# Slot 2 of a mixture-of-experts kernel: rows turned earlier, its lists split, and the last write of an item moved past a branch

## The chip, the cores and the metric

The kernel runs on 1 core of one Trainium2 chip, as one launch. The metric is the device time in microseconds; lower is better. PE is TensorE, DVE is VectorE, ACT is ScalarE, POOL is GpSimd, SP is SyncE, which here only issues DMAs.

## What is computed

Two stages in float32. First a sparse attention over q, k, v of shape (4 batches, 8 heads, 768 tokens, 64): each token sees the keys closer than 16 positions, and one summary (maximum of keys, mean of values) for every block of 32 tokens.

```
k_sum, v_sum = block max of k, block mean of v          # 24 blocks of 32
scores = [q k^T / 8 where |i-j| < 16, q k_sum^T / 8 + log 32]
x = softmax(scores) @ [v; v_sum]                        # (3072 tokens, 512)
```

Then a routed expert layer over the 3072 tokens of x: every token goes to the one expert of 8 with the largest gate logit.

```
e = argmax(x @ w_gate);  gate = softmax(x @ w_gate)[e]
out = gate * sigmoid(x @ w_output_gate)[e] * (relu(x @ w1[e]) @ w2[e])    # w1: 512x1024, w2: 1024x512
```

Which tokens belong to which expert is known only while the kernel runs.

## The kernel before

**Attention.** 24 tiles of 128 tokens (4 batches of 6). Each goes through scores on PE, mask and row minimum on DVE, subtraction on POOL, exponential on ACT, turning and weighting on PE, normalisation on DVE; the result is stored to DRAM (x_dr) and its gate logits are formed. The order of all these steps, on all engines at once, is written out by hand in the string ORDER: `sc.3:P` is the scores of tile 3 in the PSUM bank pair P, `rk.4.v` reorders a loaded block of k on DVE (`.a` ACT, `.p` POOL), `pu`, `kg` move block means, `lv` loads values, `r` is a step of routing, `sp` splits one weight tile, `ef`, `er`, `e2` are slot 0's two matrix products, `fa` builds four of the 24 "places" matrices (one-hot rows), `fr.2` gathers slot 2's rows. Each engine works through its part of the string in order.

**Slots.** Tokens of one expert are packed into slots of 256 rows. Slots 0 to 2 are formed from the first two batches while attention still runs; slots 3 to 7 follow in straight code; after that items of 256 rows (`full`) and of 128 rows (`half`) alternate inside nested run-time branches (`pairs`, `left`, `more`). In this run there are three of each, slots 8 to 13.

**One slot.** Each weight tile (128x512, 256 KB) comes by a DMA of SP into a ring of raw buffers, is rounded on ACT (w1h, w2h; line 1053) and its remainder formed on DVE (w1l, w2l; line 1054). x rows are gathered by an indirect DMA of POOL (`fetch`, line 1015) into xg, turned on PE (line 1066) and rounded likewise by `take_x` (xhl, lines 1068 and 1069). `first_wide` (lines 1100 and 1102) makes eight hidden blocks j in four PSUM banks, each evicted by ACT and DVE; `second` adds eight blocks of three matmuls for two row tiles (lines 1339 to 1341). At j = 4 of `second` the next slot's rows are turned. `write` scales the result into y and POOL scatters it to out by an indirect DMA (line 1370). In `half` y is scaled half on DVE (line 1364) and half on ACT (line 1365).

**Slot 1** (`full_with`) is ordered by hand as well. Between its products DVE does the remaining routing steps (`rest_slots`) and splits the weights of slots 1 and 2. When the table of the later slots is made, it also issues `final_match` (line 1243, on DVE: which token falls into which list, 24 x 40 entries) and POOL's `final_entries` (line 971, five products of up to 1000 elements). At j = 4 of its second product it turns slot 2's rows.

**Lists.** A slot's row numbers and gates are collected on PE: 24 matmuls of places by entries (`final_collect`, line 1264), then unpacked on DVE (lines 977 to 979). Before, one collection at block 4 of slot 2's first product serves all slots from 3 on; slot 3's rows are fetched at block 6. `few_*` treats two small leftover groups of up to 32 tokens in slots 3 to 7.

**Branches.** Every engine loads the counts and takes each branch for itself (line 1479); line 1536 is the end of the program, where all engines meet. From slot 2 on only POOL's order is as written; the other engines' orders are a scheduler's, except in `half`.

Of the kernel before, what the change touches and what calls it, by code (L numbers as in the profile page):

```python
# [11 lines left out]
F32 = mybir.dt.float32  # L12
F32R = mybir.dt.float32r
BF16 = mybir.dt.bfloat16
# [8 lines left out]
P = 128  # L23
# [40 lines left out]
lk.0 rk.0.v lk.2 lk.1 pk.0.0:P rk.1.v rk.2.a pk.0.1 kk.0 lq.0 pk.2.0:S pk.2.1 lk.3 cl.0 pk.1.0:V lq.1 lk.4 rq.0.a  # L64
pk.1.1 mk.2 mk.0 rq.1.p kk.2 rk.3.p pq.0.0:S pq.0.1 pq.1.0:S lk.5 rk.5.p kk.1 mk.1 kq.0 ks.0.v lq.2 pq.1.1 sc.0:P kq.1
rq.2.p lv.2.0.p pk.3.0:S pk.3.1 hm.16:T ma.0 sc.1:V rk.4.v kk.3 lv.0.0.s lv.1.0.s cl.1 mi.0 pk.5.0:P lv.4.0.s mk.3
ma.1 lq.3 lv.3.0.s pk.5.1 pk.4.0:V pk.4.1 sc.2:S me.0.0 lv.5.0.s su.0 lv.0.1.s mk.5 pq.2.0:S pq.2.1 mi.1 sc.3:P kk.4
ma.2 mi.2 lq.4 ex.0 kk.5 tp.0.0:S su.1 kq.2 lk.7 tp.0.1 me.0.1 rq.3.a ex.1 sc.4:V su.2 mk.4 lv.2.1.s lv.1.1.s ma.3
lq.5 kp.0 me.0.2 tp.1.0:P ex.2 mi.3 lv.9.0.s ma.4 tp.2.0:S tp.2.1 tp.1.1 ke.0 lv.3.1.s mg.0:M pq.3.0:P pq.3.1
lv.10.0.s lv.7.0.p su.3 lk.6 lq.6 kg.0.vvvv kp.1 kp.2 ex.3 ks.1.p lv.6.0.p sc.5:V lq.7 mi.4 hm.20:T kq.3 ma.5 pu.2.a  # L70
mi.5 rq.4.p tp.3.0:S pu.0.v tp.3.1 lv.5.1.s sc.6:V va.0.0:P pu.3.a va.0.1 su.4 pu.4.a va.2.0:V ex.4 va.2.1 sc.7:P
tp.4.0:S ma.6 kp.3 lv.8.0.p pq.4.0:V pq.4.1 no.0 tp.4.1 lv.6.1.s no.2 su.5 pu.1.p lk.8 ex.5 me.1.0 mi.6 tp.5.0:V
tp.5.1 ma.7 rk.7.p tx.0:P va.1.0:S va.1.1 kq.4 va.3.0:V mi.7 kp.4 va.3.1 no.1 sc.8:P lv.11.0.p tx.2:S me.1.1 kp.5
rq.5.p kx.0 kx.2 su.6 tx.1:V st.1.s pu.5.v pq.5.0:S pq.5.1 no.3 me.1.2 ex.6 tp.6.0:S kq.5 st.2.s ma.8 tp.6.1 lv.13.0.s
lv.12.0.s sc.9:V kx.1 rk.6.v lv.4.1.p pk.6.0:P st.0.p lk.9 su.7 ke.1 pk.6.1 mi.8 kp.6 tx.3:S ex.7 tp.7.0:V mg.1:M
va.4.0:S su.8 kx.3 kk.6 va.4.1 kg.1.aaaa lg.1:T tp.7.1 sc.10:P ma.9 mi.9 pk.7.0:S rq.6.p pu.6.p lv.7.1.p lv.9.1.p
st.3.s pk.7.1 kp.7 mk.6 ex.8 lv.14.0.s kl.1 va.5.0:V kk.7 va.5.1 pq.6.0:P no.4 hm.6:T pq.6.1 lg.0:T ma.10 tp.8.0:V
tp.8.1 rk.8.p pu.10.a pu.8.v lv.8.1.s su.9 no.5 va.6.0:P va.6.1 tx.4:S mk.7 kq.6 lv.17.0.s lv.15.0.s rq.7.p sc.11:V
tx.5:S kl.0 mi.10 st.5.s su.10 no.6 kp.8 lk.10 pk.8.0:P kx.4 pk.8.1 lt.0:T tx.6:S me.2.0 pq.7.0:V pu.7.p ex.9 ma.11
pq.7.1 mk.8 tp.9.0:S tp.9.1 va.7.0:P va.7.1 rk.9.v pk.9.0:V kx.5 pk.9.1 ks.2.v lv.16.0.s pu.9.v lt.1:T lq.8 kt.0 ex.10  # L80
lv.10.1.s no.7 kx.6 kk.8 tx.7:P kq.7 kt.1 mi.11 kp.9 kk.9 st.6.s sc.12:S ma.12 st.4.p su.11 mk.9 kx.7 va.8.0:P va.8.1
lg.2:T tp.10.0:S no.8 kl.2 tp.10.1 me.2.1 mi.12 va.9.0:V pu.11.v va.9.1 no.9 kp.10 sc.13:P lv.11.1.s ex.11 rk.10.p
sc.14:S ma.13 lk.11 mi.13 tp.11.0:V tp.11.1 kp.11 me.2.2 ma.14 pk.10.0:P pk.10.1 lt.2:M tx.8:S su.13 mi.14 ke.2 lg.3:T
mg.2:M va.10.0:V va.10.1 kt.2 kk.10 rq.8.p tx.9:S kl.3 st.7.s pq.8.0:P pq.8.1 kx.8 mk.10 no.10 ex.13 lt.3:T va.11.0:V
va.11.1 kx.9 kq.8 su.12 kg.2.vvvv tp.13.0:P ex.12 tp.13.1 sc.16:S tx.10:V no.11 kp.13 lg.4:M tx.11:P pu.13.v kx.10
# [814 lines left out]
class Experts:  # L900
# [296 lines left out]
    def full_with(self, s, rest):  # L1197
# [10 lines left out]
        for j in range(NF):  # L1208
            if j == 4:
                self.take_x(2)  # L1210
# [329 lines left out]
```

## Time and profile before

| | |
|---|---|
| time, median of 3 runs | 494.48 us (494.2 to 495.54) |
| profiled execution's own time | 494.04 us |
| its span, first to last instruction | 492.2 us |
| mean granted TensorE clock | 0.956 of full speed |
| busy in the span | PE 454.3 us (92%), DVE 381.2 (77%), ACT 323.6 (66%), POOL 209.4 (43%) |
| DMA | 113.78 MB, 231 GB/s on average |

The span is the profiled execution without what lies around it (1.84 us). Shares are averages over stages of different kind: attention (to 178 us), slots 0 and 1 (to 213.6), slot 2 (to 248.7), straight slots (to 375), branches. So it is read by stage.

### The profile page before, as it was taken

How to read it: one execution, taken by the hardware profiler on the slowest of the kernel's cores; microseconds unless marked ns; L12 is line 12 of the kernel's file. 1: busy time of each engine (PE TensorE's matmuls, PEld its weight loads, DVE VectorE, ACT ScalarE, POOL GpSimd, SP SyncE). 2: the span in 40 equal slices, each digit the busy share in tenths (PEclk: the TensorE clock that was granted, in tenths of full speed). 3: DMA queues.
4: the chain of work that ended last, by engine and by line, in shares of the span. 5: the costliest groups of instructions: out<-in, count | busy, mean ns of one | idle time of the engine just before them, and what ended most of it. 6: DMA issues, size and time to landing. Idle time of an engine off the chain costs nothing.

```text
span 492.2 us, 13115 instructions
## 1 busy us (share of the span) xinstructions
PE 454.3 (92%) x4647; PEld 370.0 (75%) x4647; DVE 381.2 (77%) x760; ACT 323.6 (66%) x605; POOL 209.4 (43%) x224
## 2 busy tenths in 40 slices
PE   6779899998799999949999999999999999999992
PEld 6646677676577789838888887888877888888881
DVE  1675878999886887999878786678747878978884
ACT  2466588587587664624667676667656777877773
POOL 3387955585876079655321212131202313113112
PEclk9686999999899999977999999999999999999997
DMA  9999999697148897157796962999717699598560
GB/s 229 244 202 190 210 248 238 161 222 163 57 155 306 242 381 258 68 162 244 218 355 229 397 228 82 316 390 381 252 56 271 213 307 328 180 313 318 189 218 28
DMA packets 101514, 113.78 MB, mean 231 GB/s; under 512 B 35634, under 2 KB 60388, under 8 KB 101440
## 3 DMA queue, kind: packets, MB, share of 16 engines
q1 hardware_dynamic: 94624, 94.59, 64.4%
q0 software_dynamic: 6816, 18.27, 11.3%
q8 instruction: 38, 0.62, 0.6%
q14 instruction: 36, 0.29, 0.2%
HBM read 102.70 MB, written 12.98 MB: 235 GB/s over the span
## 4 chain that ended last, share of the span: by engine, by line
PE 52%; DVE 1%; issue 1%; ACT 0%; ACTq 0%; DVEq 0%
PE bank L1100 14%; PE bank L1341 8%; PE bank L1339 8%; PE bank L1340 8%; PE bank L1102 7%; PE bank L1066 2%; PE bank L1293 1%; PE bank L1291 1%; PE bank L1292 1%; PE bank L1462 1%; PE bank L1441 1%; DVE w2l L1054 1%; PE bank L1304 1%; PE bank L1264 0%; DVE xhl L1069 0%
## 5 line engine op out<-in xcount | busy, mean ns | idle before, releaser
L1100 PE MATMUL bank<-xhl,w1h 128*128 128x512 f32 x288 | 106.2, 408 | 7.3 <-DVE xhl L1069 6.8
L1015 POOL DMA_INDIRECT xg<-x_dr,ids x32 | 39.1, 1221 | 99.7 <-PE bank L1066 84.1
L1102 PE MATMUL bank<-xhl,w1l 128*128 128x256 f32 x288 | 81.3, 284 | 0.0
L1339 PE MATMUL bank<-w2h,hh 128*128 128x512 f32 x200 | 80.3, 401 | 0.0
L1340 PE MATMUL bank<-w2l,hh 128*128 128x512 f32 x200 | 78.7, 393 | 0.0
L1341 PE MATMUL bank<-w2h,hl 128*128 128x512 f32 x200 | 77.9, 396 | 0.0
L1100 PEld LDWEIGHTS bank<-xhl,w1h 128*128 128x128 f32 x288 | 55.2, 192 | 21.5 <-DVE xhl L1069 7.2
L1054 DVE TENSOR_TENSOR w2l<-wrawb,w2h 128x512 fp32r<-128x512 f32 x77 | 53.1, 706 | 22.2 <-ACT w2h L1053 19.3
L1053 ACT ACTIVATE w2h<-wrawb 128x512 fp32r<-128x512 f32 x77 | 47.1, 627 | 21.7 <-PE bank L1341 16.4
L1102 PEld LDWEIGHTS bank<-xhl,w1l 128*128 128x128 f32 x288 | 55.6, 193 | 1.2
L492 POOL TENSOR_TENSOR pr<-pr,mn 128x960 f32<-128x960 f32 x24 | 43.2, 1805 | 20.4 <-DVE mn L487 12.0
L1370 POOL DMA_INDIRECT out_dram<-y,ids x25 | 27.7, 1109 | 55.6 <-DVE y L1367 17.0
L1053 ACT ACTIVATE w1h<-wrawb 128x512 fp32r<-128x512 f32 x73 | 42.3, 623 | 10.6 <-PE bank L1100 10.5
L1054 DVE TENSOR_TENSOR w1l<-wrawb,w1h 128x512 fp32r<-128x512 f32 x70 | 46.1, 687 | 2.3 <-ACT w1h L1053 1.0
L1054 DVE TENSOR_TENSOR w2l<-wrawa,w2h 128x512 fp32r<-128x512 f32 x43 | 34.3, 815 | 15.0 <-ACT w2h L1053 12.4
L1341 PEld LDWEIGHTS bank<-w2h,hl 128*128 128x128 f32 x200 | 37.5, 188 | 8.9 <-DVE hl L1307 0.9
L1339 PEld LDWEIGHTS bank<-w2h,hh 128*128 128x128 f32 x200 | 37.6, 188 | 7.6
L1340 PEld LDWEIGHTS bank<-w2l,hh 128*128 128x128 f32 x200 | 37.6, 188 | 7.6
L479 DVE TENSOR_TENSOR pr<-sp,c_sb 128x960 f32<-128x960 f32 x24 | 27.7, 1155 | 15.8 <-PE pt L506 8.3
L1106 ACT ACTIVATE hh<-lo 128x256 fp32r<-128x256 f32 x72 | 28.7, 413 | 16.0 <-DVE lo L1105 12.1
L1105 DVE TENSOR_TENSOR lo<-bank,lo 128x256 f32<-128x256 f32 x72 | 28.9, 418 | 10.0 <-ACT lo L1104 8.7
L1107 DVE SCALAR_TENSOR_TENSOR hl<-lo,hh 128x256 fp32r<-128x256 f32 x72 | 29.3, 421 | 8.9 <-ACT hh L1106 6.4
(261 smaller groups left out, 954.2 us busy)
## 6 DMA issues: line engine op xcount, KB each, us to landing
wrawb<-in_moe_w_dram SPq DMA_DIRECT2D x150, 256.0 KB
wrawa<-in_moe_w_dram SPq DMA_DIRECT2D x82, 256.0 KB
raw_k<-in_k_dram SPq DMA_DIRECT2D x12, 512.0 KB
raw_q<-in_q_dram SPq DMA_DIRECT2D x12, 512.0 KB
vw<-in_v_dram SPq DMA_DIRECT2D x33, 128.0 KB
w1few<-in_moe_w_dram SPq DMA_DIRECT2D x16, 256.0 KB
w2few<-in_moe_w_dram SPq DMA_DIRECT2D x16, 256.0 KB
x_dr<-xs SPq DMA_DIRECT2D x14, 256.0 KB
```

The costliest lines, as they stand in the source:

```text
L492: nc.gpsimd.tensor_tensor(pr, pr, mns.pop(i).unsqueeze(2).to_broadcast([P, H, W]), ALU.subtract)
L1015: nc.gpsimd.indirect_dma_start(out=self.xg[t], out_offset=None, in_=self.x_dr[0:rows, :], in_offset=bass.IndirectOffsetOnAxis(ap=self.entr ...
L1053: nc.scalar.activation(hi, raw, AF.Copy)
L1054: (lo_by or nc.vector).tensor_tensor(lo, raw, hi.bitcast(F32), ALU.subtract)
L1100: nc.tensor.matmul(hp.rearrange("p a n -> p (a n)"), lhsT=w_h[:, fs], rhs=self.x[:, c].rearrange("p a n -> p (a n)"), start=c == 0, stop=F ...
L1102: nc.tensor.matmul(hp[:, 1, :], lhsT=w_l[:, fs], rhs=self.xh[:, c, :], start=False, stop=c == NC - 1)
L1105: nc.vector.tensor_tensor(lo, hp[:, 0, :], lo, ALU.add)
L1106: nc.scalar.activation(hh[:, j, :], lo, AF.Relu)
L1107: nc.vector.scalar_tensor_tensor(hl[:, j, :], lo, 0.0, hh[:, j, :].bitcast(F32), ALU.max, ALU.subtract)
L1339: nc.tensor.matmul(y, lhsT=hh[:, j, tk], rhs=w_h, start=j == 0, stop=False)
L1340: nc.tensor.matmul(y, lhsT=hh[:, j, tk], rhs=w_l, start=False, stop=False)
L1341: nc.tensor.matmul(y, lhsT=hl[:, j, tk], rhs=w_h, start=False, stop=j == NF - 1)
```

## The change

1. In `full_with`, `take_x(2)` moves from j = 4 to j = 1 of the second product, and `final_match` and the five `final_entries` are no longer issued there.
2. The lists are split. Slots 3 to 5 get their own (6 columns): match and entries on DVE and the collection in slot 2, the fetch of slot 3 at block 5. The lists of all later slots (34 columns) are made later: the match on POOL as 24 operations in slot 2, the five entries on POOL one at a time in slots 2, 3 and 4, the collection in slot 4, `few_lists` there too.
3. From slot 7 on, the scatter of an item's last row tile (`y_last`, all of it scaled by ACT) is held back and issued by `send_last` inside the next item's branch, or after all branches; so are the gather of the item after next and the last one (after a full item) or three (after a half item) w2 tiles of the next item.
4. ORDER is replaced by another order of the same 792 steps. Counted by engine: copies of k and q on DVE 5 and 5, on ACT 4 and then 8, on POOL 15 and then 11; copies of means (`pu`) on ACT 11 and then 5, POOL 6 and 14, DVE 7 and 5; `kg` of one batch from DVE to ACT. The order now ends with slot 0's write ahead of the places (`fa`).

```diff
 ORDER = """
-lk.0 rk.0.v lk.2 lk.1 pk.0.0:P rk.1.v rk.2.a pk.0.1 kk.0 lq.0 pk.2.0:S pk.2.1 lk.3 cl.0 pk.1.0:V lq.1 lk.4 rq.0.a
...
-fa.0 sp.v xx.0 xx.2 fr.2 e2.4 e2.5 fa.1 fa.2 e2.6 r.3 sp.v sp.v fa.3 r.3 st.21.s fa.4 sp.v sp.v fa.5 e2.7 r.3 r.3 gp.3
-wr
+hm.6:T lk.1 lk.0 rk.0.a lk.2 rk.1.p rk.2.v lq.0 lq.1 lk.3 rk.3.p lk.4 pk.1.0:V pk.0.0:P rq.0.a pk.0.1 pk.2.0:S pk.1.1
+pk.2.1 pq.0.0:V mk.2 lk.5 pq.0.1 lv.4.0.p lv.2.0.p kk.1 kk.0 mk.1 mk.0 ks.0.v cl.1 lq.2 pk.3.0:S kk.2 lv.3.0.s pk.3.1
+rq.1.v rk.5.v pq.1.0:V kq.0 cl.0 kk.3 mk.3 pq.1.1 lv.0.0.p kq.1 rk.4.a lq.3 lv.1.0.s sc.0:P sc.1:V pk.5.0:P ma.0
...
-CF = 2 * (NITEM - 2) + SMALL
+SOON = 3
+CS = 2 * SOON
+CF = 2 * (NITEM - 2 - SOON) + SMALL
...
 (full_with)
-            if j == 4:
+            if j == 1:
                 self.take_x(2)
...
-                    self.final_match()
-                    for x in range(5):
-                        self.final_entries(x)
...
+    def soon_entries(self):
+        b = self.st.tile([P, H, D], F32, name="soon", tag="xs0", bufs=1).rearrange("p h d -> p (h d)").bitcast(BF16)
+        self.soon_b = b[:, 0:NT * NV * CS].rearrange("p (g v c) -> p g v c", v=NV, c=CS)
+        self.entries(self.tc.nc.vector, self.soon_b, self.matched("soon", slice(0, CS)), 0)
+    def soon_lists(self):
+        e = shaped(self.bank(next(self.turn)), [P, NV, CS])
+        for g in range(NT):
+            self.tc.nc.tensor.matmul(e.rearrange("p v c -> p (v c)"), lhsT=self.place_of(g),
+                                     rhs=self.soon_b[:, g].rearrange("p v c -> p (v c)"), start=g == 0, stop=g == NT - 1)
+        self.unpack(1, e)
     def final_match(self):
-        self.tc.nc.vector.tensor_tensor(self.match, self.rt["key"].unsqueeze(2).to_broadcast(sh), ...
+        for g in range(NT):
+            self.tc.nc.gpsimd.tensor_scalar(self.match[:, g, :], start, self.rt["key"][:, g:g + 1], None, ALU.is_equal)
...
+        part = [lambda x=x: self.final_entries(x) for x in range(5)]
+        return {2: {("first", 1): [self.soon_entries], ("first", 4): [self.soon_lists],
+                    ("first", 5): [lambda: self.fetch(EARLY, 2)], ("second", 0): [self.final_match], ("second", 5): [part[0]]},
+                3: {("first", 1): [part[1]], ("first", 5): [part[2]], ("second", 1): [part[3]]},
+                4: {("first", 1): [part[4]], ("first", 4): [self.final_collect, self.final_lists],
+                    ("first", 5): [self.few_lists]}}
+    def late(self, s, n):
+        return () if s < EARLY + STRAIGHT - 1 else range(NF - 1, NF) if n == 2 else range(NF - 3, NF)
...
 (write)
+            held = s >= EARLY + STRAIGHT - 1 and t == len(yp) - 1
+            y = self.y_last if held else self.mp2.tile([P, DM], F32, name="y", bufs=3)
...
+            if not held:
+                self.send(y, at)
+    def next_item(self, s, n, late):
+        if late is not None:
+            self.fetch(s + 1, 2)
+            self.fetch_w(2, s, late)
+            self.send_last()
+        self.tc.nc.gpsimd.tensor_copy(self.at_last, self.entry(s, n - 1)[0])
...
 (rest)
         self.pairs(EARLY + STRAIGHT, 0, *n)
+        self.send_last()
```

`next_item` is called at the head of `full` (from slot 7 on; slot 7 only copies its row numbers) and of `half`. `fetch(nxt2, 2)` in the middle of an item stays only in slots before 7.

## Rows read from the trace of the kernel before

**Rows 1.** Windows: length, busy us (instructions) of PE, PEld, DVE, ACT, POOL; clock; DMA share; GB/s.

```profile
0.00:50.00 50.00, 39.60 (x565) 30.77 (x565) 27.28 (x32) 26.28 (x33) 28.74 (x39) 0.76 1.05 216
...
120.00:132.00 12.00, 8.12 (x178) 5.83 (x174) 11.62 (x36) 6.21 (x8) 7.64 (x11) 0.96 0.13 37
...
190.00:213.60 23.60, 23.60 (x154) 21.27 (x152) 21.11 (x86) 13.61 (x27) 15.36 (x27) 1.00 0.29 95
...
248.70:375.00 126.30, 125.92 (x806) 104.12 (x804) 92.75 (x184) 83.80 (x182) 26.54 (x24) 1.00 0.75 266
375.00:482.60 107.60, 107.50 (x540) 89.17 (x540) 88.65 (x162) 81.30 (x169) 27.76 (x23) 1.00 0.75 255
...
222.00:225.00 3.00, 3.00 (x11) 2.52 (x11) 3.00 (x3) 0.00 (x0) 3.00 (x2) 0.50 0.83 311
```

**Rows 2.** Timeline of PE, slots 1 to 3: start, us, instruction, idle before.

```profile
213.36 0.39 PE L1341 MATMUL bank<-w2h,hl 128*128 128x512 f32 x1
220.52 0.80 PE L1100 MATMUL bank<-xhl,w1h 128*128 128x512 f32 x1 [6.77 <-DVE xhl L1069]
...
226.84 0.40 PE L1100 MATMUL bank<-xhl,w1h 128*128 128x512 f32 x1
...
229.31 1.29 PE L1264 MATMUL bank<-entries,places 128*128 128x200 bf16 x13
...
248.73 0.39 PE L1100 MATMUL bank<-xhl,w1h 128*128 128x512 f32 x1
```

**Rows 3.** Timeline of DVE, slots 1 and 2.

```profile
213.58 1.15 DVE L1243 TENSOR_TENSOR match<-key,startb 128x960 bf16<-128x960 f32 x1
...
219.79 1.27 DVE L1069 TENSOR_TENSOR xhl<-bank,xhl 128x512 fp32r<-128x512 f32 x2
...
226.86 0.74 DVE L1367 TENSOR_SCALAR y<-bank,gates 128x512 f32<-128x512 f32 x1
```

**Rows 4.** Lines of DVE, 214.5 to 226.5: count | busy us, mean ns | idle.

```profile
L1054 DVE TENSOR_TENSOR w2l<-wrawa,w2h 128x512 fp32r<-128x512 f32 x5 | 8.6, 1773 | 0.0
...
L1069 DVE TENSOR_TENSOR xhl<-bank,xhl 128x512 fp32r<-128x512 f32 x2 | 1.3, 674 | 0.0
```

**Rows 5.** Lines of POOL, 189 to 226.

```profile
L965 POOL TENSOR_SCALAR places<-c_sb,rowof 128x128 bf16<-128x128 bf16 x20 | 13.2, 672 | 0.0
L971 POOL TENSOR_TENSOR entries<-match,vals 128x1000 bf16<-128x1000 bf16 x4 | 9.0, 2286 | 8.2 <-DVE match L1243 8.2
```

**Rows 6.** Timeline of PE, from slot 3 to slot 4.

```profile
271.59 0.39 PE L1100 MATMUL bank<-xhl,w1h 128*128 128x512 f32 x1
...
272.53 0.62 PE L1341 MATMUL bank<-w2h,hl 128*128 128x512 f32 x2
```

**Rows 7.** Lines of DVE, 132 to 178: slot 0's list entries.

```profile
L971 DVE TENSOR_TENSOR entries<-match,vals 128x360 bf16<-128x360 bf16 x1 | 1.2, 1180 | 0.0
```

**Rows 8.** Timeline of PE, 140 to 143.5: the collection of the first lists.

```profile
141.16 0.47 PE L1001 MATMUL entries<-entries,places 128*128 128x30 bf16 x12
```

**Rows 9.** Lines of DVE, 189 to 206, while POOL builds places.

```profile
L1054 DVE TENSOR_TENSOR w1l<-wrawb,w1h 128x512 fp32r<-128x512 f32 x4 | 2.9, 713 | 0.0
```

**Rows 10.** Timeline of all engines at the end.

```profile
482.38 0.40 PE L1341 MATMUL bank<-w2h,hl 128*128 128x512 f32 x1
...
484.47 1.01 POOL L1370 DMA_INDIRECT out_dram<-y,ids  x1 [1.49 <-ACT y L1365]
484.75 1.90 DVE L1054 TENSOR_TENSOR w2l<-wrawa,w2h 128x512 fp32r<-128x512 f32 x3 [1.06 <-ACT w2h L1053]
```

**Rows 11.** Source views of lines 1369, 1479, 1536: ns min/median/max, first and last start.

```profile
L1369 ACT ACTIVATE y<-bank,gates x11: 670/688/690, 190.3 to 470.3; 128x512 f32<-128x512 f32 x11
...
L1479 PEldq COMPARE_BRANCH  x8: 72/145/3585, 374.7 to 483.0; - x8
...
L1479 POOLq COMPARE_BRANCH  x8: 38/42/70, 383.9 to 487.9; - x8
...
L1536 POOLq DRAIN  x3: 46/103/589, 490.7 to 491.9; - x3
```

More of the change, by code (lines that the diff above doesn't have):

```diff
@@ L69 @@
[L69 to L73, printed above, removed]
@@ L1109, in first_wide, with full @@
             self.fetch_w(1, nxt, range(j - 3, j + 1))
-    def full(self, s, nxt_n=2, steps={}):
+    def full(self, s, nxt_n=2, steps={}, late=None):
+        if s >= EARLY + STRAIGHT - 1:
+            self.next_item(s, 2, late)
         hidden = self.hidden()
@@ L1309, in half @@
         with self.tc.manual_schedule(engines={mybir.EngineType.PE, mybir.EngineType.Activation, mybir.EngineType.DVE}):
+            self.next_item(s, 1, late)
             first(0, range(4))
@@ L1329, in half @@
                     self.write(s, yp)
-                if j >= 2:
+                if j >= 2 and j - 2 not in self.late(s, 1):
                     self.fetch_w(2, nxt, [j - 2])
-            self.fetch_w(2, nxt, (NF - 2, NF - 1))
     def second_block(self, j, yp, hh, hl):
@@ L1352, in second @@
                 self.write(s, yp)
-            self.fetch_w(2, nxt, [j])
+            if j not in self.late(s, 2):
+                self.fetch_w(2, nxt, [j])
             for x in steps.get(("second", j), ()):
@@ L1369, in write, with send, send_last @@
                 nc.scalar.activation(y, yp[t], AF.Copy, scale=gate)
-            i = nc.gpsimd.indirect_dma_start(
-                out=self.out, out_offset=bass.IndirectOffsetOnAxis(ap=at, axis=0),
-                in_=y, in_offset=None, bounds_check=N - 1, oob_is_err=False)
-            self.tc.declare_no_dep(i.ins, group="rows", reason="every token is in one slot only")
-            self.tc.add_to_no_dep_group("rows", i.ins)
+            if not held:
+                self.send(y, at)
+    def send(self, y, at):
+        i = self.tc.nc.gpsimd.indirect_dma_start(
+            out=self.out, out_offset=bass.IndirectOffsetOnAxis(ap=at, axis=0),
+            in_=y, in_offset=None, bounds_check=N - 1, oob_is_err=False)
+        self.tc.declare_no_dep(i.ins, group="rows", reason="every token is in one slot only")
+        self.tc.add_to_no_dep_group("rows", i.ins)
+    def send_last(self):
+        self.send(self.y_last, self.at_last)
+    def next_item(self, s, n, late):
[4 more added lines that the diff above has]
+        self.tc.nc.gpsimd.tensor_copy(self.at_last, self.entry(s, n - 1)[0])
     def run(self):
-        steps = {2: self.final_steps()}
+        steps = self.final_steps()
         for i in range(SMALL):
@@ L1391, in few_steps @@
                  for k in range(2)]
-        if i == 0:
-            steps[0]["second", 1].append(self.few_lists)
         steps[1]["second", NF - 2].append(lambda: self.few_rows(i))
```

168 lines of the change are left out of this document (88 added, 80 removed).

## The prediction

> **What bounds the kernel now.** I read the page's busy table first, then windows by stage, then the timeline of each stage with idle time, then the end. PE bounds most of it: from 248.7 us to the last matmul it is busy 125.92 of 126.30 and 107.50 of 107.60 us at full clock, with DVE at 73% and 82% [rows 1]. Nothing that only shortens another engine's work there can count. Time is left in three places. Attention: PE idles 10.4 of the first 50 us at a mean clock of 0.76, and 3.9 us at 120 to 132, where DVE is busy 11.62 of 12.00 [rows 1]. Between slots 1 and 2: PE's last matmul of slot 1 ends at about 213.6, the next starts at 220.52 after 6.77 us of waiting for xhl on DVE, and then runs at half clock (granted 0.50, which is the 1.2 GHz level of 1.2 and 2.4) [rows 1, 2]. The end: the last matmul ends at 482.6, the span at 492.2, so 9.6 us follow in which almost nothing is computed [rows 10].
>
> **Slot 1 to slot 2.** Why is xhl late? In DVE's queue it stands behind the match (213.58) and three splits, and starts at 219.79 [rows 3]. These splits take 1.773 us, against 0.713 before; POOL runs its entries meanwhile, 2.286 us each, and only instructions with both inputs in SBUF stretch: xhl, which reads PSUM, keeps 0.674 [rows 4, 5, 9]. With take_x at block 1, xhl comes some 10 us sooner, beside PE's blocks; the match (1.15) and the entries leave this stretch. So PE goes on at 213.6.
>
> What is late next is DVE's backlog. From 213.58 the old queue still held seven splits and y; the new one holds those and, moved ahead, xhl's 1.3: 213.58 + 1.2 (xhl) + 7 x 0.61 (splits overlap by about 0.1) + 0.7 (y) = 219.8. PE needs 0.353 us for a pair of matmuls (226.84 to 229.31 is seven pairs) [rows 2], so four blocks of four pairs last 5.6 us and it wants the first bank back at 219.2. DVE adds the first block at 219.8, free at 220.2 if nothing goes ahead of it. Ahead may go two splits of slot 3 (1.3) and the new soon entries: 720 elements, by the row of 360 in 1.18 us 2.4, by 960 in 1.15 us for the match 0.9 [rows 3, 7]; its own small match adds 0.2. So the stall lies between 1.0 us and 5 us; in the latter case the clock can fall as it did after 6.77 us, and five to six us at half clock cost another 2.6 [rows 1, 2]. I take 2.5 us: one of the two ahead, and no fall.
>
> A plain slot lasts from 248.73 to 272.99 less 0.94 of the next slot's work = 23.3 us [rows 2, 6]. The soon collection is 24 matmuls of 30 columns, by 12 in 0.47 us 0.9 [rows 8]. Slot 2 ends at 213.6 + 23.3 + 0.9 + 2.5 = 240.3 instead of 248.73: 8.4 us gained.
>
> **What comes back in slots 2 to 4.** The large collection moves to slot 4, with 170 columns instead of 200: 13 in 1.07 us start to start [rows 2], so 24 x 0.082 x 0.85 = 1.7 us on PE, given back. The entries shrink to 4 x 1.94 + 1.55 = 9.3 us of POOL; by the ratio of 0.713 to 1.773, DVE loses 60% of that, 5.6 us, of which 3.5 in slot 3. DVE's spare time is 27% of 23.3, 6.2 us per slot [rows 1], which hides it; without cover it costs 5.6, at best 0. I take 0.5. The 24 comparisons on POOL are not in the trace. The places are the nearest row, 0.672 us for 128 columns [rows 5]; beside them a split keeps 0.713 [rows 9]. So POOL works 24 x 0.2 to 0.67 = 5 to 16 us, in a stage where it is four fifths idle, and DVE loses 0 to 1. The next gathers of POOL's queue stand behind the comparisons, but have a slot's length to land.
>
> Here a page speaks against the change. The Trainium skill, "SBUF — State Buffer", section "Who interferes with whom", says that a DVE instruction with two SBUF inputs and a GpSimd instruction that reads SBUF share one read port, and that the second to come waits for the whole of the first. The entries agree (1.773 us); the places, which also read SBUF, do not (0.713). What the rule would make of the comparisons is the third rival.
>
> **The end.** After the last matmul DVE and ACT scale half of y each, ACT behind DVE; POOL scatters at 484.47; DVE splits weights nobody will use until 486.65 [rows 10]. POOL's last branch starts at 487.9, its drain only at 490.7, and the program ends at 492.2: some 2.8 us pass on the jump out of the nested branches, and 1.5 after the first drain. PE's jump lasts 3.585 us, from 483.0 to 486.6 [rows 11]. POOL's branch waits 2.4 us after its scatter's 485.48; my reading, to be tested, is that it waits there for the rows to land. After the change nothing holds POOL at its last test, so it jumps while PE still multiplies. ACT alone scales y, from 482.65 for 0.688 us [rows 11], POOL scatters 0.28 later (the old gap), 483.6 to 484.6; landing by about 1.9 after that, 486.5; then the drain and the meeting of the engines, 1.5: 488.0. PE's jump would allow 487.4 (486.6 and 0.8). Gain 4.2 us. From below it can be 0.3, if POOL's jump still waits (second rival); from above 4.8, PE's jump.
>
> The other moved steps cost nothing while their cover lasts. The held scatter of an item stands behind POOL's next gathers, each about 1 us. Gathers moved to the head of an item have at least 8 us before their rows are turned, even in a half item. The late w2 tiles are used 10 us or more after the head. PE's queue there is full [rows 1]; without cover each of six heads could cost 1 us.
>
> **The written order.** Steps and their number are the same; DVE sheds about 3 us of copies, ACT 1, POOL takes on some 5. In the new order the first mask stands behind a copy of k's sixth block on DVE, the order ahead starts PE's k blocks differently, and the long wait at 120 to 132 stays, being a chain of DVE steps. No row prices this. From PE's idle time in the first 50 us I bound it by 4 us either way (about a third of 14.3 us idle in the two stretches), and take 0.
>
> **The sum.** Against the profiled execution's 494.04 us (span 492.2 and 1.84 around it): - 8.4 + 1.7 + 0.5 - 4.2 = - 10.4, so 483.6. The median of the runs is 0.44 above that execution, so the forecast is 484.1 us; its own range, with the order's bounds, 480.5 to 487.
>
> **Rivals.**
> 1. DVE's backlog takes the place of the wait. Splits and soon entries go ahead of the first addition, PE stalls 4.9 us and its clock falls: 4.9 + 2.6 instead of 2.5, so 489.1. For it: DVE is busy 21.11 of 23.60 us in slot 1 [rows 1]. Against: the bank can be freed by a 0.42 us addition the moment DVE gets there.
> 2. The held write waits for the jump. If POOL's exit waits for ACT or DVE rather than for its own rows, its jump starts after y (483.4), 0.7 and 2.8 later the scatter is issued at about 487.3, and issue, landing and drain bring the end to 491.9. The end then gains 0.3, and the time is 488.0. For it: DVE's last split ends at 486.65, also shortly before POOL's branch.
> 3. On the other side: the comparisons block DVE like the entries. Place: second half of slot 2. Price: 24 x 0.672 x 60% = 9.7 us of DVE. DVE's work in slot 2 is then 17.1 (73% of 23.3) + 2.6 (soon) + 0.5 (unpacking) + 1.2 (one entries) + 9.7 = 31.1, from 219.8 to 250.9, 10.6 us behind the forecast's 240.3; with one fall of the clock 13.2, so 497.3, slower. It decides once DVE loses more than 10.4 us in all beyond the forecast. Against it stands 0.713 us beside the places.
> 4. The order costs more than its bounds, about 9 us, so 493.1; or it gives more than 4, below 480.5. For it: two stretches of half clock in attention could become three.
>
> **How the numbers follow.** Forecast 0.50, rival 1 0.18, rival 2 0.15, rival 3 0.05, rival 4 0.07 worse and 0.05 better. The range 480.0 to 490.5 leaves out rivals 3 and 4, 0.17. A difference under 0.3%, about 1.5 us, can't be told from none here. Faster: 0.50 + 0.18 + 0.15 + 0.05 = 0.88. The worse side of rival 4 lies on the bound: 0.04 same, 0.03 slower. With rival 3: same 0.04, slower 0.08.
>
> **What would show it.** Right: PE's gap before slot 2's first matmul under 1 us and a stall of 1 to 3 us at its fifth block, clock 1.0; slot 3 starting near 240 if attention ends as before; splits of 1.7 us only beside the five entries; POOL's last branch ahead of the last scatter, and 5 to 6 us from the last matmul to the end. Wrong: POOL's scatter later than 486 us less the earlier gains (rival 2); splits of over 1 us beside the comparisons (rival 3); slot 1's first matmul away from 190.1 by more than 4 us (the order). The prediction as a whole fails if slot 3 starts less than 3 us earlier relative to slot 1.

## The result and the profile after: slower by 0.6%

The changed kernel takes 498.86 us, median of 20 runs (493.45 to 504.32), beside 493.37 us for the kernel before (20 runs on the same chip, 489.51 to 498.92). The ratio is 1.0062 with a 95% interval of 1.0034 to 1.009; the medians differ by 1.1%. In a second comparison the ratio was 1.0122 (1.0035 to 1.0209). The ratios leave out a kernel's slow runs, those over 1.5% above its fastest, and the medians do not, so where the two differ both are given. The forecast was 484.1, faster, with a range of 480.0 to 490.5.

The changed kernel was profiled twice. What follows is read from the second profile (span 498.6 us, own time 500.39); the first (504.21) shows the same waits, of 7.50 us for slot 4's rows instead of 7.35.

The simplest ruler is the moment at which ACT scales the last row tile of each slot (y): it ends a slot. Timeline of ACT in the kernel before (start, us, instruction, idle before), slots 0, 2 and 6:

```profile
190.34 0.69 ACT L1369 ACTIVATE y<-bank,gates 128x512 f32<-128x512 f32 x1 [0.72 <-PE bank L1341]
...
248.93 0.69 ACT L1369 ACTIVATE y<-bank,gates 128x512 f32<-128x512 f32 x1 [0.77 <-PE bank L1341]
...
346.68 0.69 ACT L1369 ACTIVATE y<-bank,gates 128x512 f32<-128x512 f32 x1 [0.77 <-PE bank L1341]
```

The same in the kernel after:

```profile
197.41 0.69 ACT L1401 ACTIVATE y<-bank,gates 128x512 f32<-128x512 f32 x1 [0.72 <-PE bank L1374]
...
246.77 0.69 ACT L1401 ACTIVATE y<-bank,gates 128x512 f32<-128x512 f32 x1 [0.65 <-PE bank L1374]
...
357.01 0.69 ACT L1401 ACTIVATE y<-bank,gates 128x512 f32<-128x512 f32 x1 [0.77 <-PE bank L1374]
```

So in these profiles attention and slot 0 end 7.1 us later; slots 1 and 2 take 49.4 us instead of 58.6 (-9.2); slots 3 to 6 take 110.2 instead of 97.8 (+12.5); what follows takes 141.6 instead of 145.5 (-3.9). The sum is +6.4, the difference of the spans (498.6 and 492.2). Two of the four terms came as forecast; two are losses that the forecast took as about nothing.

Windows of after (columns as in [rows 1]). The stretch from 240 to 268 us, where before had PE busy throughout, holds two windows with idle PE, and the clock falls in the second. The single line below them, for comparison, is before's window from 140 to 160 us:

```profile
0.00:50.00 50.00, 35.89 (x471) 25.37 (x472) 24.57 (x26) 24.06 (x33) 29.36 (x45) 0.80 1.11 213
120.00:132.00 12.00, 11.36 (x260) 7.73 (x260) 11.04 (x37) 8.73 (x11) 10.59 (x19) 1.00 0.53 162
140.00:160.00 20.00, 13.12 (x267) 10.59 (x260) 12.05 (x21) 10.08 (x14) 10.98 (x10) 0.91 0.69 222
...
220.00:240.00 20.00, 18.63 (x116) 15.21 (x115) 18.25 (x50) 11.02 (x26) 6.31 (x7) 1.00 0.76 260
240.00:256.00 16.00, 12.45 (x66) 10.09 (x64) 13.97 (x27) 11.74 (x25) 15.18 (x24) 1.00 0.99 337
256.00:268.00 12.00, 8.19 (x37) 6.95 (x38) 2.16 (x3) 2.49 (x6) 5.67 (x5) 0.72 0.59 223
268.00:300.00 32.00, 32.00 (x180) 26.79 (x179) 29.24 (x58) 21.22 (x48) 9.36 (x8) 1.00 0.75 254
```

```profile
140.00:160.00 20.00, 17.97 (x368) 14.35 (x366) 13.71 (x28) 16.82 (x25) 13.54 (x14) 1.00 0.82 283
```

PE's timeline of after, answering to [rows 2]: slot 2 follows slot 1 without a gap, one stall of 1.33 us remains, and then PE waits 7.35 us for slot 4's rows and goes on at half clock (a pair of matmuls every 0.64 us instead of 0.35, for five pairs):

```profile
220.45 0.40 PE L1374 MATMUL bank<-w2h,hl 128*128 128x512 f32 x1
220.69 0.40 PE L1107 MATMUL bank<-xhl,w1h 128*128 128x512 f32 x1
...
230.41 0.50 PE L1372 MATMUL bank<-w2h,hh 128*128 128x512 f32 x1 [1.33 <-DVE y L1399]
...
252.17 0.28 PE L1109 MATMUL bank<-xhl,w1l 128*128 128x256 f32 x1
259.81 0.66 PE L1073 MATMUL bank<-id_sb,xg 128*128 128x128 f32 x2 [7.35 <-DMA xg<-x_dr,ids]
260.12 0.78 PE L1107 MATMUL bank<-xhl,w1h 128*128 128x512 f32 x1
260.69 0.41 PE L1109 MATMUL bank<-xhl,w1l 128*128 128x256 f32 x1
260.91 0.63 PE L1107 MATMUL bank<-xhl,w1h 128*128 128x512 f32 x1
```

When PE asks for these rows matters. The scheduler put slot 4's first transposes into the middle of slot 3's first product, here at 252.4 us, 8 us behind the start of the turning of slot 3's rows (244.30). It had done so in before too, 9.4 us after the second gather of those rows (244.98). PE's timeline of before:

```profile
254.42 0.31 PE L1066 MATMUL bank<-id_sb,xg 128*128 128x128 f32 x1
```

POOL's timeline of after shows why the rows are late. The 24 comparisons run for 14.39 us behind slot 3's gathers; slot 4's two gathers come behind them, at 253.04 and 254.62, when PE is already waiting. POOL then starts nothing for 6.2 us, and slot 2's writes leave 17 us after their y:

```profile
237.44 1.02 POOL L1022 DMA_INDIRECT xg<-x_dr,ids  x1 [0.31 <-issue]
238.50 14.39 POOL L1274 TENSOR_SCALAR match<-startb,key 128x34 bf16<-128x34 f32 x24
253.04 1.27 POOL L1022 DMA_INDIRECT xg<-x_dr,ids  x1 [0.16 <-issue]
254.62 1.02 POOL L1022 DMA_INDIRECT xg<-x_dr,ids  x1 [0.30 <-issue]
261.85 1.61 POOL L976 TENSOR_TENSOR entries<-match,vals 128x850 bf16<-128x850 bf16 x1 [6.21 <-issue]
263.62 1.06 POOL L1407 DMA_INDIRECT out_dram<-y,ids  x1 [0.15 <-issue]
```

DVE's lines, 238 to 252 us: beside the comparisons a split keeps its 0.685 us, as beside the places [rows 9]:

```profile
L1061 DVE TENSOR_TENSOR w1l<-wrawb,w1h 128x512 fp32r<-128x512 f32 x6 | 3.9, 685 | 1.1 <-ACT w1h L1060 1.1
```

The end, answering to [rows 10]: timeline of all engines.

```profile
492.18 0.39 PE L1374 MATMUL bank<-w2h,hl 128*128 128x512 f32 x1
492.39 0.69 DVE L1061 TENSOR_TENSOR w2l<-wrawa,w2h 128x512 fp32r<-128x512 f32 x1
492.66 0.69 ACT L1401 ACTIVATE ylast<-bank,gates 128x512 f32<-128x512 f32 x1 [0.66 <-ACT w2h L1060]
494.21 0.99 POOL L1407 DMA_INDIRECT out_dram<-ylast,atlast  x1 [9.17 <-ACTq L1526]
```

POOL's branches, answering to [rows 11] (ns min/median/max, first and last start): the last starts at 486.8, before the last write and while PE multiplies. From the last matmul's end (492.6) to 498.6 pass 6.0 us instead of 9.6.

```profile
L1526 POOLq COMPARE_BRANCH  x8: 38/42/65, 389.9 to 486.8; - x8
```

### The profile page after: what moved, and what is told of

Its sections match the earlier page's. It is cut to its first block, busy times and chain, and to the rows that moved or that the text cites. A ratio compares the mean times of both kernels' runs of the same rounds, so it can differ in the third digit from the quotient of the medians.

```text
span 502.4 us, 13158 instructions
## 1 busy us (share of the span) xinstructions
PE 459.3 (91%) x4671; PEld 372.3 (74%) x4671; DVE 371.0 (74%) x752; ACT 321.1 (64%) x604; POOL 230.3 (46%) x263
## 5 line engine op out<-in xcount | busy, mean ns | idle before, releaser
L1107 PE MATMUL bank<-xhl,w1h 128*128 128x512 f32 x288 | 104.8, 403 | 0.6 <-issue 0.5
L1374 PE MATMUL bank<-w2h,hl 128*128 128x512 f32 x200 | 76.4, 394 | 0.0
L1061 DVE TENSOR_TENSOR w2l<-wrawb,w2h 128x512 fp32r<-128x512 f32 x77 | 51.8, 689 | 21.9 <-ACT w2h L1060 18.2
L1022 POOL DMA_INDIRECT xg<-x_dr,ids x30 | 34.6, 1154 | 65.1 <-PE bank L1073 53.1
L1061 DVE TENSOR_TENSOR w1l<-wrawb,w1h 128x512 fp32r<-128x512 f32 x70 | 47.9, 714 | 4.7 <-ACT w1h L1060 4.0
L1111 ACT ACTIVATE lo<-bank 128x256 f32<-128x256 f32 x72 | 27.0, 378 | 27.0 <-PE bank L1109 19.1
L1407 POOL DMA_INDIRECT out_dram<-y,ids x18 | 20.6, 1143 | 42.3 <-DVE y L1399 18.0
L1061 DVE TENSOR_TENSOR w2l<-wrawa,w2h 128x512 fp32r<-128x512 f32 x40 | 30.4, 780 | 9.1 <-ACT w2h L1060 8.7
```

Of the source, the lines that this page charges most:

```text
L1022: nc.gpsimd.indirect_dma_start(out=self.xg[t], out_offset=None, in_=self.x_dr[0:rows, :], in_offset=bass.IndirectOffsetOnAxis(ap=self.entr ...
L1061: (lo_by or nc.vector).tensor_tensor(lo, raw, hi.bitcast(F32), ALU.subtract)
L1107: nc.tensor.matmul(hp.rearrange("p a n -> p (a n)"), lhsT=w_h[:, fs], rhs=self.x[:, c].rearrange("p a n -> p (a n)"), start=c == 0, stop=F ...
L1374: nc.tensor.matmul(y, lhsT=hl[:, j, tk], rhs=w_h, start=False, stop=j == NF - 1)
```

## The experiments

All kernels by the same ruler (slot 0's last y; slots 1 and 2; slots 3 to 6; from there to the last instruction; us, from one profile each), with the ratio to before:

| kernel | slot 0 | 1-2 | 3-6 | rest | ratio (95%) |
|---|---|---|---|---|---|
| before | 190.3 | 58.6 | 97.8 | 145.5 | 1 |
| after, second profile | 197.4 | 49.4 | 110.2 | 141.6 | 1.0122 (1.0035-1.0209) |
| e1 after, old order | 191.3 | 49.4 | 109.7 | 141.4 | 0.9937 (0.9906-0.9967) |
| e2 after, comparisons behind gathers | 197.7 | 49.4 | 106.9 | 141.8 | 1.0000 (0.9963-1.0037) |
| e3 both | 192.7 | 49.4 | 108.4 | 141.9 | 0.9925 (0.9885-0.9964) |
| e4 before, new order | 194.7 | 59.0 | 97.8 | 145.5 | 1.0110 (1.0061-1.0159) |
| f1 e1, one comparison on DVE | 189.4 | 54.0 | 97.4 | 141.6 | 0.9845 (0.9780-0.9910) |
| f2 e1, comparisons in slot 1 | 192.2 | 53.9 | 100.8 | 141.2 | 0.9869 (0.9811-0.9928) |
| f4 before, early turning | 187.0 | 59.8 | 97.5 | 145.2 | 0.9994 (0.9959-1.0030) |
| f5 before, branches' part | 190.0 | 57.5 | 97.8 | 141.6 | 0.9875 (0.9837-0.9913) |
| g1 after, two means on ACT | 195.3 | 49.5 | 108.2 | 142.2 | 0.9891 (0.9845-0.9938) |
| g3 f1 without drain | 193.0 | 53.7 | 100.8 | 141.5 | 0.9913 (0.9859-0.9967) |
| g4 f1, comparison in slot 3 | 194.1 | 54.1 | 98.3 | 141.6 | 0.9867 (0.9832-0.9901) |
| h1 g4 with the mended new order | 191.4 | 55.1 | 98.9 | 141.3 | 0.9881 (0.9805-0.9956) |
| h2 before, mended new order | 188.3 | 59.0 | 97.8 | 145.1 | 0.9971 (0.9925-1.0017) |

In the row of after the columns are of the second profile and the ratio is that of the second comparison. By the medians the ratio of g1 is 1.000, that of f5 0.991 and that of e4 1.017.

The border between slots 2 and 3 is soft: the scheduler can put work of slot 3 ahead of slot 2's end. So the sum of slots 1 to 6 is compared: 156.3 before, 159.6 after.

Kernels that share their code in a stretch, or nearly, show how steady the ruler is. The nine profiles with the old order have slot 0's end anywhere from 187.0 to 194.1 us, so a single one is good to some 3.5 us; the four with the new order unmended have 194.7 to 201.0, 6.6 us later on average. The other columns repeat better: 97.5 to 97.8 for slots 3 to 6 in before, e4, f4, f5 and h2, and 141.2 to 142.2 for the rest wherever the last write is held back.

**The order and the place of the comparisons.** e1 puts the old ORDER string back; e4 gives the new one to the kernel before; e2 moves one step; e3 does both e1 and e2.

```diff
-("second", 0): [self.final_match], ("second", 5): [part[0]]
+("second", 4): [self.final_match], ("second", 5): [part[0]]
```

e1: 

> The kernel after with one thing undone: the written order of attention and slot 0 is that of before; slot 1's early turning, the split lists and the held writes stay. The trace of after showed slot 1's first matmul at 200.8 us instead of 190.1, slot 2 without the gap, a wait of 7.5 us for slot 4's rows and 6.0 us after the last matmul instead of 9.6. Theory A (the order costs some 10 us of attention, the comparisons of the later lists cost some 9 us because slot 4's gathers queue behind them on POOL, the rest gains): slot 1's first matmul back at 190 +-1.5, the wait for slot 4's rows still there; time 10 us below after, about 489, so 0.99 of before. Rival B (the order is neutral, and attention is later in that one profile for another reason): slot 1's first matmul at 196 or later, and the time within 3 us of after. Rival C (the wait for the rows is a matter of that profile alone): attention as in A, but no wait over 3 us in slot 3, time about 480.

e2: 

> The kernel after with one thing moved: the 24 comparisons on POOL stand behind slot 4's gathers (at block 4 of slot 2's second product) instead of ahead of them (at block 0). Same work, same order of attention. Theory A: slot 4's gathers are issued about 14 us earlier, PE doesn't wait for the rows and its clock stays at full speed; 8 to 10 us below after, about 490. Rival B (the order is neutral and the wait is the whole loss): also 8 to 10 us below after, but then e1 gains nothing. Rival C (the comparisons hold back something else, DVE's splits or the next write): under 3 us below after, with waits for DVE or POOL in slot 3 in place of the one for the rows.

e3: 

> The kernel after with both: the written order of before, and the 24 comparisons behind slot 4's gathers. What is left of the change is the early turning, the split lists and the held writes. Theory A: the two losses are separate, so they add up: about 480 (494 less 9 for the gap, less 4 for the end, plus 1 to 2 for the collections), 0.97 of before. Rival (a loss remains that neither explains, for example the entries on POOL slowing DVE's splits in slots 3 and 4): 485 or more.

e4: 

> The kernel before with the written order of after and nothing else. Theory A: slot 1's first matmul some 10 us later, near 200.8, and the time 8 to 11 us above before, 1.016 to 1.022 of it. Rival B: within 3 us of before. If slot 1 starts 10 us later but the time rises by clearly less, something in slots 1 and 2 takes up part of it.

Medians: e1 491.98, e2 493.68, e3 491.95, e4 502.30, before 494.11. The order costs 1.1% in the kernel before and about as much in after: rival B falls. By the ratio that is less than the 1.6% that theory A gave as the least. The other half of theory A held only in part. In e1 slot 4's rows are late again, by 2.85 us, just under rival C's 3, and the collection waits 2.78 us for the entries; rival C's time of 480 did not come. In e2 and e3 the rows are in time (0.30 us of waiting and none), yet slots 3 to 6 still take 107 to 108 us, and e3's time is its rival's, over 485, not the 480 of theory A. What is late instead is shown by ACT's timeline of e3:

```profile
264.57 0.63 ACT L1061 ACTIVATE w2h<-wrawb 128x512 fp32r<-128x512 f32 x1 [1.35 <-PE bank L1375]
273.28 0.69 ACT L1402 ACTIVATE y<-bank,gates 128x512 f32<-128x512 f32 x1 [8.08 <-DMA out_dram<-y,ids]
```

ACT waits 8.08 us to fill a buffer of y, of which the change left three instead of four (what a fourth would do here was not run). POOL's timeline of e3 shows slot 2's writes behind the comparisons, 24 us after their y (made at 242.1):

```profile
251.09 13.68 POOL L1275 TENSOR_SCALAR match<-startb,key 128x34 bf16<-128x34 f32 x24 [8.44 <-issue]
264.73 1.61 POOL L977 TENSOR_TENSOR entries<-match,vals 128x850 bf16<-128x850 bf16 x1
266.50 1.35 POOL L1408 DMA_INDIRECT out_dram<-y,ids  x1 [0.16 <-issue]
```

So it is not one place: ahead of the gathers the comparisons make rows late, behind them they make writes late. That 14 us of comparisons do not fit into POOL's slot at all was the next theory.

**POOL's time, and the parts alone.** f1 makes the match on DVE; f2 moves the 24 comparisons ahead of slot 1's writes; f4 and f5 are parts of the change in the kernel before (f5 is point 3 of the change).

```diff
 f1 (final_match)
...
-        for g in range(NT):
-            self.tc.nc.gpsimd.tensor_scalar(self.match[:, g, :], start, self.rt["key"][:, g:g + 1], None, ALU.is_equal)
+        self.match = self.matched("match", slice(CS, CS + CF))
 f2 (full_with)
+        self.final_match()
         self.write(s, yp)
 f2 (final_steps)
-("second", 0): [self.final_match], ("second", 5): [part[0]]
+("second", 5): [part[0]]
 f4 (full_with)
-            if j == 4:
+            if j == 1:
                 self.take_x(2)
```

f1: 

> The kernel after with the written order of before, and the 24 comparisons on POOL (13.7 to 14.5 us there) replaced by one comparison of all 24 x 34 entries on DVE at the same place, as before had it (by its row of 960 elements in 1.15 us about 1.0 us). So far every version that keeps the 24 comparisons lost 9 to 12 us between the ends of slots 2 and 6, wherever they stood: ahead of slot 4's gathers PE waited for the rows, behind them ACT waited 6.4 to 8.1 us for a buffer of y whose write stood behind them. Theory A (it is POOL's time: 14 us of comparisons do not fit beside its gathers, the wait behind them and its writes): both waits go, slots 3 to 6 take 98 to 101 us from end to end instead of 108 to 110, time about 483 to 485, 0.98 of before. Rival B (it is the entries on POOL, which stretch DVE's splits to 1.66 us, or the collection in slot 4): slots 3 to 6 still take 106 or more, time about 490.

f2: 

> The kernel after with the written order of before, and the same 24 comparisons on POOL moved to the end of slot 1's second product, ahead of its writes, where POOL idled 16.9 us before the first write (207 to 224 us in the version with the old order). Theory A (POOL's time where it is short is the loss): slots 3 to 6 take 98 to 101 us, time about 483 to 485; the first write of slot 1 at most 2 us later. Rival B as for the version with one comparison on DVE: 106 us or more. Rival C (comparisons in this place slow slot 1's splits, where DVE is 89% busy): slots 1 and 2 take more than 51 us from the end of slot 0 instead of 49.4.

f4: 

> The kernel before with one line changed: slot 2's rows are turned at block 1 instead of block 4 of slot 1's second product. Match, entries and the one collection stay where they were. Theory A (the split of the lists was needed because the match and the splits of 1.77 us keep DVE): the wait of 6.8 us for xhl goes, but PE waits 4 to 6 us for the first bank in slot 2; slots 1 and 2 take 53 to 57 us instead of 58.6, time 489 to 493. Rival (the early turning alone does it): about 50 us, time about 486.

f5: 

> The kernel before with the part on the branches alone: the last write of an item held back behind the next test, the gathers and last w2 tiles at the head of an item, y on ACT alone, three buffers of y instead of four. Theory A: 3.7 to 4.2 us off the end and nothing else, 0.992 of before: from the end of slot 6 to the last instruction 141 to 142 us instead of 145.5. Rival (POOL's jump still waits, or the heads of the items cost PE time): under 1.5 us.

Medians: f1 486.49, f2 486.57, f4 493.24 and f5 488.53, before 493.08. With f1 slots 3 to 6 fall to 97.4 us, below the bound that theory A gave. Slots 1 to 6 take 151.4, 4.9 less than before. Rival B falls: the entries and the collection in slot 4 are still there. ACT's timeline of f1, the last y of slots 0 and 6:

```profile
189.44 0.69 ACT L1399 ACTIVATE y<-bank,gates 128x512 f32<-128x512 f32 x1 [0.72 <-PE bank L1372]
...
340.82 0.69 ACT L1399 ACTIVATE y<-bank,gates 128x512 f32<-128x512 f32 x1 [0.77 <-PE bank L1372]
```

Against f1 the comparisons on POOL cost 7.6 us of slots 1 to 6 where e1 has them (159.0), 6.5 in e3 (157.9) and 3.2 in f2 (154.6). In time f2 can't be told from f1 (0.9869 and 0.9845; both medians lie about 1.5 us above theory A's range). So the theory holds for slot 2, but not for POOL's time as such: at the end of slot 1, where POOL had idled for 16.93 us in e1, most of the cost goes. What is left in f2 has a cause in its trace: POOL could start the comparisons only at 217.3, when the last of the tables was ready, so slot 1's first write left 5.9 us later than in e1, counted from slot 0's end (2 were expected), slot 3's gathers stood behind it, and PE waited 1.99 us for the rows. Slots 1 and 2 pass rival C's 51 us with 53.9, but f1, which has no comparisons on POOL, takes 54.0; so that row speaks neither for nor against rival C. f4 is a miss for its rival, since early turning alone gains nothing, and for the sizes of theory A too: slots 1 and 2 took 59.8 us, not 53 to 57, and the wait was longer than 6 us. PE's and then DVE's timeline of f4:

```profile
225.86 0.80 PE L1100 MATMUL bank<-xhl,w1h 128*128 128x512 f32 x1 [8.02 <-DVE lo L1105]
```

```profile
211.45 1.15 DVE L1243 TENSOR_TENSOR match<-key,startb 128x960 bf16<-128x960 f32 x1
212.52 9.76 DVE L1054 TENSOR_TENSOR w2l<-wrawa,w2h 128x512 fp32r<-128x512 f32 x5
222.20 2.61 DVE L1054 TENSOR_TENSOR w2l<-wrawb,w2h 128x512 fp32r<-128x512 f32 x2
```

The wait for xhl becomes a wait of 8.02 us for the first bank, behind the match and splits of 1.95 us beside the entries. So the early turning needs the lists out of slot 1. f5 shows the branches' part by itself: 3.9 us less behind slot 6. In time it is 1.25% (0.87 to 1.63) by the ratio, 6.2 us, and 0.9% or 4.6 us by the medians, which is closer to those 3.9 us.

**What the order costs, and a better place.** g0 is after again; g1 changes two steps of its order, g3 drops the drain behind the gathers, g4 moves f1's comparison.

```diff
 g1 (ORDER)
-... pu.20.p ... pu.22.p ...
+... pu.20.a ... pu.22.a ...
 g3 (second, j == 4)
-                self.tc.nc.gpsimd.drain()
 g4 (final_steps)
-("second", 0): [self.final_match], ("second", 5): [part[0]]},
-3: {("first", 1): [part[1]], ("first", 5): [part[2]], ("second", 1): [part[3]]},
+},
+3: {("first", 0): [self.final_match], ("first", 1): [part[0]], ("first", 3): [part[1]],
+    ("first", 5): [part[2]], ("first", 7): [part[3]]},
```

g0: 

> The kernel after, unchanged, for a profile beside the others. Theory A: the three terms show again: slot 0's last write made 4 to 11 us later than in before (190.3 us), slots 3 to 6 some 9 to 13 us longer than before's 97.8, the stretch behind slot 6 near 142 us instead of 145.5; PE waits 4 to 8 us for slot 4's rows. Rival: the wait for the rows is not there in another profile.

g1: 

> The kernel after with two steps of the written order on another engine: the copies of two means of batch 3 (pu.20 and pu.22), which the new order gave to POOL behind slot 0's gathers, go to ACT. In every profile with the new order these copies started only 6.0 to 7.8 us after the gathers, and PE waited 4.7 to 6.0 us for them; in before POOL's next instruction started at once. Theory A (that wait is most of what the order costs): the wait of PE at 151 to 157 us goes or falls under 1.5 us, slot 0's last write is made 4 to 6 us earlier than in after's other profiles, time 4 to 6 us below after. Rival (the order's loss lies in its first 50 us, where the clock falls for another reason, and the wait only hides what DVE would do next): under 2 us.

g3: 

> The kernel after with the order of before and the one comparison on DVE, and without the drain that POOL executes behind the gathers at block 4 of a second product. After these gathers POOL started nothing for 5.7 to 9.1 us in all profiles. Theory (the drain holds POOL until the gathers are through): POOL's next instruction follows within 1.5 us, the writes of y go out 6 to 8 us earlier; the time stays within 2 us of the same kernel with the drain, 486.5, since nothing on PE's path waits there any more. Rival (POOL waits for something else): the 6 to 9 us stay.

g4: 

> The kernel after with the order of before, the one comparison on DVE moved from slot 2 to the head of slot 3, and four of the five entries one by one in slot 3's first product. In the version with the comparison in slot 2 DVE ran it at 217.2 us, inside the backlog that PE waits for. Theory A: slots 1 and 2 take 50 to 52 us instead of 54.0, slots 3 to 6 stay at 97 to 99, time 484 to 486, the fastest so far. Rival (entries closer together stretch the splits of slot 3, or the collection in slot 4 waits for the last): slots 3 to 6 take 101 or more.

Medians: g0 497.89, g1 492.83, g3 489.81, g4 485.39, before 492.96. g0 shows all three terms, so its rival falls. g1 is 5 us below g0 by the medians, and level with before. Its 14 runs spread from 483.84 to 499.64, and its ratio to before (0.989) and that of the medians (1.000) disagree, so the size is less sure than the trace: the wait of PE fell from 4.97 to 0.86 us. POOL's timeline of g0 shows that wait's cause, the copies of means start 5.93 us behind the gathers:

```profile
146.14 1.04 POOL L1022 DMA_INDIRECT xg<-x_dr,ids  x1 [0.30 <-issue]
153.11 2.02 POOL L334 COPY vw<-mst 24x1024 f32<-24x1024 f32 x2 [5.93 <-DMA xg<-x_dr,ids]
```

and PE's timelines of g0 and then of g1 show who waits for it:

```profile
154.20 2.11 PE L522 MATMUL pv<-vw,pT 120*64 120x65 f32 x34 [4.97 <-POOL vw L334]
```

```profile
152.31 2.95 PE L522 MATMUL pv<-vw,pT 120*64 120x65 f32 x93 [0.86 <-ACT vw L336]
```

The wait was 4.69 to 5.95 us in all four profiles with these copies on POOL (after twice, e2, e4), and 0.86 to 1.33 in the three with them on ACT (g1, h1, h2).

In g3 POOL's next instruction follows the gathers at once (242.83, behind 241.82 + 1.00), so it was the drain that held POOL there; its rival falls. The time did not gain by it, and the forecast that it would stay within 2 us of f1 missed: 489.81 is 3.3 above f1's median of 486.49, though the two were run in different comparisons. Slots 3 to 6 took 100.8 us instead of 97.4, with a wait of PE of 2.23 us for hl, a result of DVE, just behind three entries in a row. POOL's timeline of g3:

```profile
241.82 1.00 POOL L1023 DMA_INDIRECT xg<-x_dr,ids  x1 [0.30 <-issue]
242.83 1.64 POOL L977 TENSOR_TENSOR entries<-match,vals 128x850 bf16<-128x850 bf16 x1
```

g4 came to the forecast time of its theory but not by its path: slots 1 and 2 did not shorten (54.1), slots 3 to 6 stayed at 98.3. It beats both kernels (12 runs, 483.27 to 491.07); its lead over f5 alone (0.9867 and 0.9875) can't be told from nothing.

**Both causes out, nothing undone.** h1 is g4 with the new order as mended in g1; h2 is the kernel before with that order.

h1: 

> The kernel after with both causes taken out and nothing undone: the new written order with the copies of the two means on ACT, and the match of the later lists as one comparison on DVE at the head of slot 3 (entries in slot 3's first product). If the wait behind slot 0's gathers and the 24 comparisons are the whole of what the change lost: slot 0's last write near 190 to 195 us, slots 1 to 6 in about 152.4 as with the old order, 142 behind; time 483 to 488, as the version with the old order (485.4). If the rest of the new order costs too: 490 or more. If it gains, as the low end of the version with the means on ACT alone hints (483.8): under 483.

h2: 

> The kernel before with the new written order and the two copies of means on ACT. The new order alone cost 5 to 8 us against before (1.011). Theory A (the wait behind the gathers is what it costs): within 2 us of before, 0.996 to 1.004. Rival (half of it lies in the first 60 us, by the clock): still 3 us or more above before, 1.006 and up.

Medians: h1 488.67, h2 492.43, before 492.90. h2 lies at 0.9971 (0.9925 to 1.0017), e4 at 1.0110: with two steps on another engine the new order costs nothing that can be measured, so its cost was those two copies behind the gathers. The first 60 us were not the reason: h1 has the same first 50 us as after (PE busy 35.46 and 35.89 us, clock 0.80 in both) and still ends slot 0 at 191.4. h1, which keeps the whole change but these two things, is faster than before by 1.2% (0.4 to 2.0; 0.9% by the medians). It is not the sum that was expected: 488.67 lies 0.7 us above the range given, slots 1 to 6 took 154.0 us and not 152.4, and h1 is no faster than f5, which has the branches' part alone.

## Why the prediction was wrong, step by step

**Slot 1 to slot 2, forecast -8.4: right in the profile.** It was -9.2 us; the stall at the fifth block was 1.33 us, near its lower bound of 1.0, not 2.5, and the clock stayed at 1.00. Rival 1 did not come. The gain is seen in the profiles alone: f1 and g4, which keep it, are not measurably faster than f5, which lacks it.

**The end, forecast -4.2: right.** It was -3.9 us in the profiles of after and f5. The step inside it was a little short: the write follows y by 0.86 us, not 0.28, because it also waits for ACT's own branch (ACTq in its row). Rival 2 did not come; POOL's branch ran 7 us ahead of the last write.

**What comes back in slots 2 to 4, forecast +2.2: this step failed.** "So POOL works 24 x 0.2 to 0.67 = 5 to 16 us, in a stage where it is four fifths idle" and "the next gathers of POOL's queue stand behind the comparisons, but have a slot's length to land". The work was sized well (14.4 us, 0.60 each) and so was DVE's loss (none: 0.685 us beside them, so rival 3's price was wrong). Two things failed. The first is the slot's length: PE asked for slot 4's first rows 7 us after it had turned slot 3's (245.3), and before's own trace already had this place (254.42). In e2, with nothing in between, slot 4's first gather starts 0.2 us after slot 3's rows are turned; in after it starts 7.7 us after, and PE waits 7.35 us. The second is the word idle. Of a slot's 23.3 us POOL spends some 2.4 on gathers, 2.4 on writes and, by the source view of its drain, a median of 5.8 in after and 7.9 in before in that, all in order; 14.4 more is longer than what is left. So when the comparisons stood behind the gathers they held back writes and with them buffers of y. By the control f1 the comparisons cost 159.6 - 151.4 = 8.2 us in after; the wait of 7.35 and about 1.4 at half clock behind it (five pairs at 0.64 instead of 0.35) come to 8.8. Without them slots 1 to 6 take 4.9 us less than before, where the forecast's terms say 6.2 less; the 1.3 between is not taken apart.

**The written order, forecast 0 within 4: this step failed too.** It cost 1.1% (0.6 to 1.6) in e4, 5.4 us (8.2 by the medians), beyond its bounds. "No row prices this" left out what could be read without a row: the whole diff has `pu.20.p` and `pu.22.p` as POOL's next steps behind `fr.0`, where before has subtractions (`su`), and the string names the engine. The question to ask of POOL's part was what a copy of a loaded tile does behind gathers on the same engine; before's trace has no copy directly behind a gather, so the price of some 6 us could not be read there. I bounded the order from PE's idle time in the first 50 us and at 120 to 132, and the loss came at 148 to 154: of the 20 us from 140, PE is busy 13.12 in after and 17.97 in before. Rival 4's direction came true; its 9 us lie above the ratio's 5.4 and near the medians' 8.2. Its reason did not hold: the clock was lower there (0.91, before 1.00), but it is 0.91 in h1 too, which ends slot 0 at 191.4 without the wait.

**Rival 3 and the page.** Rival 3's time, 497.3, is close to what was measured, but by luck: its mechanism, DVE held up by the comparisons, did not come. A split with two SBUF inputs keeps 0.685 us beside comparisons, and takes 4.60 us beside three entries in a row (below). The Trainium skill, "SBUF — State Buffer", section "Who interferes with whom", has the second instruction wait for the whole of the first. The entries agree and go further; the comparisons, which also read SBUF, do not.

What stays open: whether anything of f5's gain lies outside the end, why the early turning with the lists out of the way (f1, g4) shows 3 to 4 us less than f5 for slots 1 to 6 in the profiles but nothing measurable in time, and what makes a copy wait behind gathers where a subtraction does not.

## What to carry to other kernels

Idle time of an engine is not free time: look at what it stands in (a drain, a wait for its own gathers), and at how much work per period its queue holds already, before adding 14 us to it. Each gather and write that an engine issues is part of its queue, so work placed ahead of one delays rows or buffers. Moving it behind only changed which, until it stood where the engine had been idle and little behind it was needed soon (f2). Before calling a gather's slack a slot's length, look up in the trace where its rows are first read. When a written order changes, read for each engine what now stands directly behind a gather.

## What the runs showed of the hardware that was not expected

POOL's drain behind two gathers lasts 4.4 us at the least, 5.8 in the median and 13.4 at the most in after (source view of line 1383, nine drains); without it, in g3, the next instruction starts at once. Where no drain stands, a copy of means still waited 5.9 to 7.8 us behind gathers in the four profiles with the new order unmended, while a subtraction there started at once (before, g1) and the same copies on ACT did not hold PE up for more than 1.33 us.

Twenty-four comparisons of 34 columns took 0.57 to 0.62 us each on POOL, nearly the 0.672 of 128 columns [rows 5]: between these two widths the price hardly changes.

Entries that follow each other on POOL held up one DVE instruction for nearly the whole run of them. DVE's timeline of after, beside three entries (265.98, 4.76 us):

```profile
266.69 4.60 DVE L1061 TENSOR_TENSOR w2l<-wrawa,w2h 128x512 fp32r<-128x512 f32 x1 [1.22 <-ACT w2h L1060]
```

and DVE's timeline of g4, beside four entries in a row (255.87, 6.33 us):

```profile
255.87 6.61 DVE L1115 SCALAR_TENSOR_TENSOR hl<-lo,hh 128x256 fp32r<-128x256 f32 x1
```

Without entries beside them the same forms take 0.69 and 0.42 us (means of before from 256 to 370 us).
